# Sixteen outer rows for wq and the FFN up weights, and a gate load of which 896 columns come in two transfers of their own

## The chip, the cores and the metric

The kernel runs on one core of a Trainium2 chip. The metric is the device time in microseconds (us) of one execution. Most executions of one kernel agree within a few tenths of a per cent (30 of the 37 runs of the kernel before lie within 0.35% of 120.8 us, all of them at 120.45 to 121.83); some are slower (two of six of the changed kernel) and are then marked slow, and a single run has an unknown state. Times are compared between fast runs. The "span" of a profiled run is what its trace covers, about 2 us less than its time (118.8 of 121.36 us for the kernel before).

## The reference, cut to what matters

It is one decode step: layer norm, attention over the last 1024 positions of a cache, and a gated FFN, multiplied together.

```python
x  = A_x                                   # 8 x 1 x 512, bf16
xn = _layernorm(x)
q  = xn @ wq                               # wq 512 x 4096
# ... softmax(q k^T) v over the last 1024 positions, 8 KV heads of 128 ...
s  = o @ wo                                # wo 4096 x 512
g  = _silu((_gelu(xn @ w_gate) * (xn @ w_up)) @ w_down)   # gate, up 512 x 1792
return x + s * g
```

With one token per sequence there is little arithmetic for each byte. The bytes are 4.2 MB of wq, 33.6 MB of K and V, 5.5 MB of FFN weights (gate, up and down) and 4.2 MB of wo, 47.46 MB in all, and every one is read once.

## The kernel before

A load of wq, gate or up gives each of the 128 partitions four consecutive rows of the weight (`k=NDC`, NDC is 4), so a partition's piece is one contiguous run in HBM: 16 KB for half of wq's columns of those rows, 14 KB for gate or up.

```python
wq_rows = A_wq.rearrange("(p k) n -> p (k n)", k=NDC)

def load_wide(rows, c0, c1):
    t = wide_slot()
    nc.sync.dma_start(out=t[:, 0 : c1 - c0], in_=rows[:, c0:c1])
    return t

def load_wq(h):                            # h = 0, 1: half of each partition's run
    return load_wide(wq_rows, h * 2 * Hq * Dh, (h + 1) * 2 * Hq * Dh)

def load_up(w):                            # gate and up
    return load_wide(w.rearrange("(p k) n -> p (k n)", k=NDC), 0, NDC * F)
```

A K or V tile holds four heads, `HN`. Its source is already in two levels, 32 outer rows by 4 heads of 8 KB each:

```python
def load_kv(cache, b, i):
    t = slot()
    nc.sync.dma_start(out=t, in_=cache[b, i*HN:(i+1)*HN, win0:Sk, :].rearrange(
        "n (p r) d -> p n (r d)", r=NKR))
    return t
```

The row order of the weights has to be the order of the contracted elements of the normalised input, which is transposed in four steps:

```python
nc.vector.tensor_scalar(out=xhat, in0=x_sb, scalar1=mv[:, 0:1], scalar2=rstd[:, 0:1], ...)
for k in range(NDC):
    nc.tensor.transpose(xT_ps[:, k, :],
                        xhat.rearrange("b (p k) -> b k p", k=NDC)[:, k, :],
                        ident[0:32, 0:32])
```

All large loads are issued by one queue, in this order: first half of wq, a K tile, second half of wq, a K tile, then V and K tiles in turn, and at the end gate, up, down and wo in six pieces from large to small. Tiles free up behind the computation, and the loads wait for them.

The softmax here doesn't subtract the row's maximum and nothing guards it: scores larger than these inputs give would overflow.

Of the kernel before, what the change touches and what calls it, by code (L numbers as in the profile page):

```python
# [16 lines left out]
def kernel(  # L17
# [13 lines left out]
    nc = tc.nc  # L31
# [7 lines left out]
    F = B_w_gate.shape[1]  # L39
    NDC = D // 128  # L40
# [4 lines left out]
    P = nc.NUM_PARTITIONS  # L45
# [33 lines left out]
    def wide_slot():  # L79
        return wide.tile([P, 2 * SLOT], BF16, name="wide_slot", align_bytes=512)  # L80
# [5 lines left out]
    x_sb = persist.tile([32, D], BF16, name="x_sb")  # L86
# [3 lines left out]



    wq_rows = A_wq.rearrange("(p k) n -> p (k n)", k=NDC)

    def load_wide(rows, c0, c1):
        t = wide_slot()
        nc.sync.dma_start(out=t[:, 0 : c1 - c0], in_=rows[:, c0:c1])
        return t

    def load_wq(h):  # L100
# [4 lines that stand above are left out]
        nc.sync.dma_start(  # L105
            out=t,
            in_=cache[b, i * HN : (i + 1) * HN, win0:Sk, :].rearrange(
                "n (p r) d -> p n (r d)", r=NKR
            ),
        )  # L110
        return t

    def load_up(w):
        return load_wide(w.rearrange("(p k) n -> p (k n)", k=NDC), 0, NDC * F)

    def load_down():
        return load_wide(B_w_down.rearrange("(p j) d -> p (j d)", j=FR), 0, FR * D)
# [4 lines left out]
    def load_wo(j0, j1):  # L122

        if (j1 - j0) * D > SLOT:
            return load_wide(wo_rows, j0 * D, j1 * D)
        t = slot()
        nc.sync.dma_start(out=t[:, 0 : (j1 - j0) * D], in_=wo_rows[:, j0 * D : j1 * D])
        return t
# [14 lines left out]
    for t in range(2):  # L143
        c = slice(t * D // 2, (t + 1) * D // 2)
# [6 lines left out]
        out=ident,  # L151
        in_=ident,
# [8 lines left out]
        out=perm.rearrange("p (h q) -> p h q", q=P // 32),  # L161
        in_=ident.rearrange("p (q h) -> p h q", q=P // 32),
# [9 lines left out]
        out=hot.rearrange("n r (m j) -> n r m j", m=HN),  # L172
        in_=hot.rearrange("n r (m j) -> n r m j", m=HN),
# [9 lines left out]
        out=far.rearrange("n (c m) -> n c m", m=HN),  # L183
        in_=far.rearrange("n (c m) -> n c m", m=HN),
# [9 lines left out]
        out=selq,  # L194
        in_=ident.rearrange("p (m q) -> p q m", q=QW),
# [5 lines left out]
        out=selr.rearrange("p r q -> p (r q)"),  # L201
        in_=ident.rearrange("p (u c) -> p c u", u=4),
# [10 lines left out]
    nc.vector.reciprocal(out=rstd, in_=rstd)  # L213
    xhat = persist.tile([32, D], BF16, name="xhat")
    nc.vector.tensor_scalar(  # L215
        out=xhat,
        in0=x_sb,
        scalar1=mv[:, 0:1],
        scalar2=rstd[:, 0:1],
        op0=ALU.subtract,  # L220
# [3 lines left out]
    for k in range(NDC):  # L224
        nc.tensor.transpose(  # L225
            xT_ps[:, k, :],
            xhat.rearrange("b (p k) -> b k p", k=NDC)[:, k, :],
            ident[0:32, 0:32],
        )
    xT = persist.tile([P, NDC, 32], BF16, name="xT")  # L230
# [20 lines left out]
    def turn_k(g, t):  # L251

        kp = ps_t.tile([P, 4 * P], FP32, name="t_ps", tag="t")
        kw = k_t[g].bitcast(FP32)
        for c in range(4):
            rp = 4 * t + c
            nc.tensor.transpose(  # L257
                kp[:, c * P : (c + 1) * P], kw[:, rp * P : (rp + 1) * P], ident_f
            )
        if t == 0:  # L260
            kT_t[g] = kT_pool.tile([P, NKR * P], BF16, name="kT")
        copy = nc.scalar.copy if t == 1 else nc.vector.tensor_copy
        copy(out=kT_t[g][:, t * 8 * P : (t + 1) * 8 * P], in_=kp.bitcast(BF16))  # L263
# [3 lines left out]
    def score(g):  # L267

        b, i = groups[g]
        sc = ps_sc.tile([P, 512], FP32, name="sc_ps")  # L270
        sc_t[g] = sc
        kT = kT_t[g].rearrange("w (r k e) -> w r k e", k=P, e=2)
        nc.tensor.matmul(  # L273
            sc,
            hot.rearrange("n r q -> n (r q)"),
            far,
            start=True,
            stop=False,
            skip_group_check=True,
        )  # L280
        for e in range(2):
            for t in range(4):
                nc.tensor.matmul(  # L283
                    sc[32 * t : 32 * t + 32, :],
                    q2_all[:, i, b, e, :, :, :].rearrange("w r n j -> w (r n j)"),
                    kT[:, :, 32 * t : 32 * t + 32, e],
                    start=False,
                    stop=(e == 1),
                    skip_group_check=True,
                    tile_position=(0, 32 * t),  # L290
                )

    def soft(g):
        p = p_pool.tile([P, 512], BF16, name="p")
        acc = small.tile([P, 1], FP32, name="acc")
        nc.scalar.activation(  # L296
            out=p, in_=sc_t[g], func=ACT.Exp, scale=inv_sqrt_dh, accum_out=acc
        )
        p_t[g] = p, acc

    def turn_p(g):
        p, acc = p_t[g]
        pT = pT_pool.tile([P, 512], BF16, name="pT")
        nc.vector.transpose(out=pT, in_=p)  # L304
        pT_t[g] = pT
        if g % 2 == 0:
            ss_t[g] = small.tile([P, 2, QW], FP32, name="ss")
        nc.vector.tensor_scalar(
            out=ss_t[g - g % 2][:, g % 2, :], in0=selq, scalar1=acc[:, 0:1], scalar2=None, op0=ALU.mult
        )  # L310

    def values(g):

        o_ps = ps_o.tile([P, 2 * Dh], FP32, name="o_ps")
        for m in range(NKR // 2):
            u = m % 4
            nc.tensor.matmul(  # L317
                o_ps[32 * u : 32 * u + 32, :],
                pT_t[g][:, m * 32 : (m + 1) * 32],
                v_t[g][:, m * 256 : (m + 1) * 256],  # L320
                start=(m < 4),
                stop=(m >= NKR // 2 - 4),
                skip_group_check=True,
                tile_position=(0, 32 * u),
            )
        o_sb = o_pool.tile([P, 2 * Dh], FP32, name="o_sb")
        nc.scalar.copy(out=o_sb, in_=o_ps)  # L327
        o_t[g] = o_sb
# [81 lines left out]
    for i in range(NHALF):  # L410
        for rr in range(2):
            copy = nc.scalar.copy if rr else nc.vector.tensor_copy
            copy(
                out=q_sb[:, i, :, :, rr, :],
                in_=q_ps[i].rearrange("p (j w e) -> p j e w", j=rep, e=2),
            )
    for i in range(NHALF):
# [8 lines left out]
        for e in range(2):  # L426
            for rr in range(2):
                copy = nc.scalar.copy if rr else nc.vector.tensor_copy
                copy(  # L429
                    out=q2_all[64 * rr : 64 * rr + 64, i, :, e, rr, :, :].rearrange(  # L430
                        "p b n j -> p j n b"
                    ),
                    in_=qT_ps[64 * rr : 64 * rr + 64, :, e, :, 0:32:NQ],
# [82 lines left out]
    for g in range(NGR + 1):  # L516
        if g < NGR:
            v_t[g] = load_kv(A_v_cache, *groups[g])
            if g + 2 < NGR:
                k_t[g + 2] = load_kv(A_k_cache, *groups[g + 2])  # L520
        if g == NGR - 1:
            wg_t = load_up(B_w_gate)
            wu_t = load_up(B_w_up)
            wd_t = load_down()
        if g == NGR:

            parts = [(0, 16), (16, 24), (24, 28), (28, 30), (30, 31), (31, 32)]
            wo_t = [load_wo(*q) for q in parts[:2]]
            for t in range(2):
                r = slice(16 * t, 16 * t + 16)  # L530
                nc.sync.dma_start(out=x_res[r, :], in_=x_rows[r, :])
            wo_t += [load_wo(*q) for q in parts[2:]]
        if g < NGR:
            score(g)
            soft(g)
        if g + 1 < NGR:
            turn_k(g + 1, 0)
        if g < NGR:
            turn_p(g)
        if g + 1 < NGR:  # L540
            turn_k(g + 1, 1)
        if g:
            values(g - 1)
        if g + 1 < NGR:
            turn_k(g + 1, 2)
            turn_k(g + 1, 3)
        if g and g % 2 == 0:
            gather(g - 2)
# [11 lines left out]
    for pair in [(j, j + 1) for j in range(0, NOR - 2, 2)] + [(NOR - 2,), (NOR - 1,)]:  # L560
        for q in range(NQ):
            for j in pair:
                a = side[j]
                rows = [m for m in range(NOR) if side[m] == a]
                piece, j0 = where[j]
                c0 = (j - j0) * D + q * DQ
# [17 lines left out]
        out=out.flatten_outer_dims().rearrange("b (q c) -> (b q) c", q=NQ), in_=out_sb  # L584
# [31 lines left out]
```

## Time and profile before

| | before |
|---|---|
| time, median of 3 | 120.66 us (120.59 to 120.96) |
| span of the profiled run | 118.8 us |
| second half of wq landed; q matmuls start | 15.46 us; 15.50 us |
| gate landed | 97.11 us |
| up landed | 101.35 us |
| last piece of wo landed | 115.50 us |
| duration of a data packet: 16 KB, 14 KB, 8 KB | 611, 535, 309 ns |

### The profile page before, as it was taken

What the parts mean: (1) busy time and instruction counts of PE and PEld (TensorE: products, weight loads), DVE (VectorE), ACT (ScalarE), POOL (GpSimd) and SP (SyncE); (2) the same over time, 40 slices, a digit from 0 to 9 for tenths busy, and PEclk for the clock granted to TensorE, in tenths of its full rate; (3) what the DMA queues carried; (4) which work ended last, traced back from release to release, by engine and by line L of the source; (5) the groups of instructions that cost most, each with busy time, mean ns of one, the idle gap of its engine ahead of it and who ended that gap; (6) DMA issues with size and microseconds to landing.
All of it is one profiled execution on the core that took longest, in us unless ns stands there. A gap on an engine that the chain in (4) does not pass through costs nothing.

```text
span 118.8 us, 2378 instructions
## 1 busy us (share of the span) xinstructions
PE 86.6 (73%) x985; PEld 59.4 (50%) x985; DVE 62.0 (52%) x131; ACT 40.5 (34%) x78; POOL 4.8 (4%) x14
## 2 busy tenths in 40 slices
PE   0005946786989899799799798778959661898680
PEld 0004713653657567577477386456638340334670
DVE  5025645543756856956866764846728336420111
ACT  5000324792442552462462462442524303002000
POOL 5900000000000000000000000000000000000000
PEclk9999999555899999999999999999999996579999
DMA  4999999999999999999999999999999999999950
GB/s 88 437 394 436 419 433 425 422 433 419 428 428 430 422 417 436 417 430 428 419 422 436 425 417 433 428 425 425 422 428 446 419 449 415 440 438 400 409 193 3
DMA packets 6345, 47.61 MB, mean 401 GB/s; under 512 B 816, under 2 KB 1088, under 8 KB 1344
## 3 DMA queue, kind: packets, MB, share of 16 engines
q1 hardware_dynamic: 6304, 47.47, 95.3%
q8 instruction: 7, 0.11, 0.3%
q14 instruction: 2, 0.02, 0.0%
q10 hardware_dynamic: 32, 0.01, 0.0%
HBM read 47.46 MB, written 0.01 MB: 400 GB/s over the span
## 4 chain that ended last, share of the span: by engine, by line
DMA 58%; PE 24%; DVE 7%; ACT 4%; SPq 2%; issue 1%; DVEq 0%
DMA wide_slot<-in_B_w_gate_dram 18%; DMA slot<-in_A_v_cache_dram 16%; DMA slot<-in_A_wo_dram 12%; DMA wide_slot<-in_A_wq_dram 11%; PE t_ps L257 11%; DVE kT L263 4%; PE sc_ps L283 4%; PE o_ps L317 3%; ACT q_all L429 2%; PE a_ps L344 2%; DVE q_all L429 2%; PE big L567 1%; ACT L296 1%; PE sc_ps L273 1%; PE big L445 1%
## 5 line engine op out<-in xcount | busy, mean ns | idle before, releaser
L263 DVE COPY kT<-t_ps 128x1024 bf16<-128x1024 bf16 x48 | 31.7, 688 | 23.3 <-PE t_ps L257 21.4
L257 PE MATMUL t_ps<-ident_f,slot 128*128 128x128 f32 x256 | 38.3, 300 | 2.4 <-DMA slot<-in_A_k_cache_dram 2.2
L257 PEld LDWEIGHTS t_ps<-ident_f,slot 128*128 128x128 f32 x256 | 31.1, 153 | 12.5 <-issue 7.6
L263 ACT COPY kT<-t_ps 128x1024 bf16<-128x1024 bf16 x16 | 16.2, 1012 | 11.6 <-ACT p L296 5.0
L296 ACT ACTIVATE p<-sc_ps 128x512 bf16<-128x512 f32 x16 | 9.6, 597 | 30.1 <-PE sc_ps L283 30.0
L283 PE MATMUL sc_ps<-kT,q_all 128*32 128x512 bf16 x128 | 10.7, 406 | 7.6 <-DVE kT L263 5.8
L304 DVE STREAM_TRANSPOSE pT<-p 128x512 bf16<-128x512 bf16 x16 | 11.2, 703 | 2.7 <-ACT p L296 2.7
L317 PE MATMUL o_ps<-slot,pT 128*32 128x256 bf16 x256 | 9.9, 275 | 1.1 <-DVE pT L304 1.1
L344 PE MATMUL a_ps<-selr,o_sb 128*128 128x16 f32 x64 | 8.4, 263 | 0.0
L283 PEld LDWEIGHTS <-q_all 128*32 128x32 bf16 x128 | 2.0, 95 | 12.4 <-DVE kT L263 8.4
L344 PEld LDWEIGHTS a_ps<-selr,o_sb 128*128 128x128 f32 x64 | 7.8, 192 | 0.0
L225 PE MATMUL t_ps<-ident,xhat 32*128 32x32 bf16 x4 | 0.3, 194 | 10.3 <-DVE xhat L215 10.3
L317 PEld LDWEIGHTS <-pT 128*32 128x32 bf16 x256 | 5.4, 95 | 4.2 <-issue 2.5
L327 ACT COPY o_sb<-o_ps 128x256 f32<-128x256 f32 x16 | 6.0, 377 | 1.3 <-PE o_ps L317 1.3
L273 PE MATMUL sc_ps<-far,hot 4*128 4x512 bf16 x16 | 6.4, 398 | 0.0
L445 PE MATMUL big<-wide_slot,xT 128*32 128x448 bf16 x32 | 2.6, 463 | 4.3 <-DMA wide_slot<-in_B_w_up_dram 3.1
L225 PEld LDWEIGHTS <-xhat 32*128 32x128 bf16 x4 | 0.2, 114 | 10.2 <-DVE xhat L215 10.2
L567 PEld LDWEIGHTS <-og 128*32 128x32 bf16 x128 | 4.1, 97 | 2.2 <-issue 1.1
L366 PE MATMUL t_ps<-q_sb,ident 128*32 128x512 bf16 x14 | 4.8, 497 | 0.0
L353 DVE RECIPROCAL rs<-a_ps 128x32 f32<-128x32 f32 x8 | 2.9, 358 | 3.0 <-PE a_ps L344 3.0
L429 DVE COPY q_all<-t_ps 64x128 bf16<-64x128 bf16 x4 | 2.7, 778 | 2.4 <-ACT q_all L429 1.6
L429 ACT COPY q_all<-t_ps 64x128 bf16<-64x128 bf16 x4 | 2.7, 726 | 2.5 <-DVE q_all L429 2.5
(70 smaller groups left out, 54.2 us busy)
## 6 DMA issues: line engine op xcount, KB each, us to landing
slot<-in_A_k_cache_dram SPq DMA_DIRECT2D x16, 1024.0 KB, 19.6
slot<-in_A_v_cache_dram SPq DMA_DIRECT2D x16, 1024.0 KB, 19.6
wide_slot<-in_A_wq_dram SPq DMA_DIRECT2D x2, 2048.0 KB, 10.6
wide_slot<-in_A_wo_dram SPq DMA_DIRECT2D x1, 2048.0 KB, 12.3
wide_slot<-in_B_w_gate_dram SPq DMA_DIRECT2D x1, 1792.0 KB, 21.4
wide_slot<-in_B_w_up_dram SPq DMA_DIRECT2D x1, 1792.0 KB, 23.2
wide_slot<-in_B_w_down_dram SPq DMA_DIRECT2D x1, 1792.0 KB, 25.0
slot<-in_A_wo_dram SPq DMA_DIRECT2D x1, 1024.0 KB, 14.4
```

The lines of the kernel that those rows point to most:

```text
L257: nc.tensor.transpose(kp[:, c * P : (c + 1) * P], kw[:, rp * P : (rp + 1) * P], ident_f)
L263: copy(out=kT_t[g][:, t * 8 * P : (t + 1) * 8 * P], in_=kp.bitcast(BF16))
L273: nc.tensor.matmul(sc, hot.rearrange("n r q -> n (r q)"), far, start=True, stop=False, skip_group_check=True,)
L283: nc.tensor.matmul(sc[32 * t : 32 * t + 32, :], q2_all[:, i, b, e, :, :, :].rearrange("w r n j -> w (r n j)"), kT[:, :, 32 * t : 32 * t + ...
L296: nc.scalar.activation(out=p, in_=sc_t[g], func=ACT.Exp, scale=inv_sqrt_dh, accum_out=acc)
L304: nc.vector.transpose(out=pT, in_=p)
L317: nc.tensor.matmul(o_ps[32 * u : 32 * u + 32, :], pT_t[g][:, m * 32 : (m + 1) * 32], v_t[g][:, m * 256 : (m + 1) * 256], start=(m < 4), st ...
L327: nc.scalar.copy(out=o_sb, in_=o_ps)
L344: nc.tensor.matmul(a_ps[:, 1, m, :], o_t[g + m][:, r * Dh : (r + 1) * Dh], selr[:, r, :], start=(r == 0), stop=(r == 1), skip_group_check= ...
L366: nc.tensor.matmul(idle[0:32, :], ident[:, 0:32], moving[:, 0:512], start=True, stop=True, skip_group_check=True,)
L429: copy(out=q2_all[64 * rr : 64 * rr + 64, i, :, e, rr, :, :].rearrange("p b n j -> p j n b"), in_=qT_ps[64 * rr : 64 * rr + 64, :, e, :, 0 ...
L567: nc.tensor.matmul(acc[a], shifted(og, j, q), wo_t[piece][:, c0 : c0 + DQ], start=(j == rows[0] and q == 0), stop=(j == rows[-1] and q == ...
```

## The change

The intent was balance. When gate lands, eight of the DMA engines finish up to 1.4 us later than the other eight. A transfer whose outer dimension is 8 runs on eight engines only (in the trace of the kernel before each load of the 8 rows of x leaves 8 completion marks), so some bytes of the gate weight were to be given to one set of eight. To get an outer dimension of 8 over 64 partitions, the rows of wq, gate and up take another order: partition `8a + c` holds the four rows that start at `(16c + a) * 4`. The source of a 128-partition load then has 16 outer rows by 8.

```diff
-    wq_rows = A_wq.rearrange("(p k) n -> p (k n)", k=NDC)
+    def blocks(w):
+        return w.rearrange("(c a k) n -> a c (k n)", c=8, k=NDC)
+
+    wq_rows = blocks(A_wq)
 ...
-        nc.sync.dma_start(out=t[:, 0 : c1 - c0], in_=rows[:, c0:c1])
+        nc.sync.dma_start(out=t[:, 0 : c1 - c0], in_=rows[..., c0:c1])
 ...
-    def load_up(w):
-        return load_wide(w.rearrange("(p k) n -> p (k n)", k=NDC), 0, NDC * F)
+    def load_up(w, low=0):
+        rows, n = blocks(w), NDC * F
+        t = load_wide(rows, 0, n - low)
+        if low:
+            for a in range(0, 16, 8):
+                nc.sync.dma_start(
+                    out=t[8 * a : 8 * a + 64, n - low : n], in_=rows[a : a + 8, :, n - low : n]
+                )
+        return t
 ...
-        out=xhat,
-        in0=x_sb,
+        out=xhat.rearrange("b (k a c) -> b c a k", a=16, c=8),
+        in0=x_sb.rearrange("b (c a k) -> b c a k", a=16, c=8),
 ...
-            xhat.rearrange("b (p k) -> b k p", k=NDC)[:, k, :],
+            xhat[:, k * P : (k + 1) * P],
 ...
-            wg_t = load_up(B_w_gate)
+            wg_t = load_up(B_w_gate, 896)
```

The bytes and the shapes of the matmuls stay the same. So does the length of each contiguous run, except that gate's 14 KB runs are cut into 12.25 and 1.75 KB.

## The prediction

Passages that rest on more than this case's traces and runs are cut out of the recorded texts, here and below, and the cuts are marked. "Low" engines are my name for the eight that carry the loads of the 8 rows of x, "high" for the other eight; no record numbers an engine, so that another load of 8 or of 4 rows runs on the same ones was not shown.

> **What bounds the kernel now.** I read the shares of the 40 slices first. The engines' row of busy time (tensor engine 73%, VectorE 52%) names no bound; the DMA row does.
>
> ```profile
> DMA  4999999999999999999999999999999999999950
> GB/s 88 437 394 436 419 433 425 422 433 419 428 428 430 422 417 436 417 430 428 419 422 436 425 417 433 428 425 425 422 428 446 419 449 415 440 438 400 409 193 3
> ...
> HBM read 47.46 MB, written 0.01 MB: 400 GB/s over the span
> ```
>
> All 16 DMA engines are over 90% busy from the second slice to the 38th, at some 425 GB/s. All of the 47.46 MB has to come in; nothing but the last landing and what follows it sets the end. The chain of work that ended last, in order of time, says what follows:
>
> ```profile
> 99.92 14.42 DMA slot<-in_A_wo_dram
> 114.33 0.04 issue
> 114.37 1.56 PE big L567 x32
> 115.94 0.02 issue
> 115.96 0.29 DVE tmp L581
> 116.25 0.02 issue
> 116.27 0.28 DVE out_sb L582
> ```
>
> The last pieces of wo arrive, matmuls that consume them piece by piece, two VectorE operations, the store: a tail of about 3.3 us after the last landing. The matmuls had waited for each piece just before:
>
> ```profile
> 114.37 1.55 PE L567 MATMUL big<-slot,og 128*32 128x128 bf16 x32 [0.32 <-DMA slot<-in_A_wo_dram]
> ```
>
> So a nanosecond on the DMA engine that finishes last is a nanosecond on the kernel, and the mean over engines does not matter. The gate load itself (the chain charges it 21.41 us) is queueing: it was issued at 75.69 and landed at 97.11, and the tensor engine sat 1.18 us idle for it there, but what waits on it (the GELU) is done long before the last wo piece (the FFN's result is ready at 110.5).
>
> Therefore I looked **engine by engine**. Each transfer leaves up to 16 completion marks in the trace's semaphore records, one per DMA engine. For the second wq load they lie within 0.3 us. For the gate load eight lie at 95.42 to 95.68 us and eight at 96.16 to 97.11; for the last wo piece eight at 113.90 to 114.13 and eight at 114.60 to 115.50. Half of the engines run about 1.4 us late, half are idle that long at the end. What makes them late is in the queue table and the packet records:
>
> ```profile
> q1 hardware_dynamic: 6304, 47.47, 95.3%
> q8 instruction: 7, 0.11, 0.3%
> q14 instruction: 2, 0.02, 0.0%
> q10 hardware_dynamic: 32, 0.01, 0.0%
> ```
>
> The seven packets of q8 are 16 KB each and start at 27.2, 42.0, 54.1, 67.0, 81.8, 92.5 and 112.3 us. Each hits one engine: it takes 0.95 us, and the data packet behind it 0.76 to 0.85 us in place of 0.31, so that engine is about 1.4 us late ever after. The number of late marks grows with them: 1 after the first, 3 after the second (a q14 packet of 8 KB came 0.5 us before it), and 8 by 97 us.
>
> [...]the x_sb loads of 8 rows show 8 data completions, and their 16 packets of 512 B on q10 fall on 8 engines.[...] No record of this trace holds addresses[...].
>
> **The change part by part.**
>
> *Intent.* In the new row order the last 896 columns have a source of 8 outer rows by 8, [...]both transfers run on the eight low engines. That takes bytes from the high eight and gives them to the low eight. It pays if the high eight are the late ones.
>
> *Are they?* I followed each engine through the packet records: a packet starts 3 or 4 ns before the end of the one before it, so chains of packets can be strung together, and the eight that carry the q10 packets are the low ones. Of the eight late engines at the gate landing, I get low ones for the fetches at 54.1 and 67.0 us and for the q14 packet at 41.5; high ones for 27.2, 42.0, 81.8 and 92.5; the q14 packet at 60.4 is ambiguous (two chains in the same phase). So three or four low engines and four or five high ones are late. The split is not low against high. The last landings of the low late ones and of the high late ones are equal to within about 0.3 us.
>
> *Cost per engine.* Median packet times are 46 ns for 1024 B, 84 for 2048, 309 for 8192 and 535 for 14336, with 3 ns of overlap. By interpolation (an estimate) 1792 B steps by 71 ns and 12544 B by 467. Gate on one engine before: 8 x 532 + 6 (completion) = 4.26 us. After, a low engine: 8 x 467 + 16 x 71 + 18 = 4.89 us, that is **+0.63 us**; a high engine: 8 x 467 + 6 = 3.74, **-0.52 us**. The late high engines gain half a microsecond, the late low ones lose 0.63, and the end follows the low ones: +0.3 (if they are the earlier of the late) to +0.63, my middle +0.5 us.
>
> *Issue.* Two more issues on the sync queue at about 0.4 us each. At this point that queue has waited 2 us per issue for a completion and then 16.2 us for the gate tile, so nothing shows. The eight completion semaphores are handed out in turn; the two small loads push up and down two turns (some 5 us) later, to about 83 and 85.5 us, still 15 us ahead of their data. The two last wo pieces still wait for up and down, as before. Nothing.
>
> *Row order.* The same bytes in rows of the same length (16 KB of wq, 14 KB of up); packet count: 128 gate packets of 14336 B become 128 of 12544 and 128 of 1792. The K and V loads already have a two-level source (32 by 4) and run at 309 ns for 8 KB, full rate. So no loss from a strided source is expected. The xhat operation (0.40 us, at 9.8 us) writes through a four-level pattern; even at three times that, xT is ready 0.8 us later and the first transposes of K (at 10.65) slip, but the q matmuls wait for the second wq half at 15.50, and DMA has the bound anyhow. Nothing.
>
> Sum: 120.66 + 0.5 = **121.1 us**.
>
> **Rivals.** *The low engines are early, as the change assumes.* Then every late engine gains 0.52 and the early ones stay below them (1.4 > 0.63 + 0.52): 120.1 us. For it: the split is exactly eight and eight. Against: my tracking, in which the engines of 54.1 and 67.0 us are clear low ones with no near neighbour of the other kind just before the fetch. It could also come true if the fetches fall on other engines in other executions, which one trace cannot show.
>
> [...]wq, gate and up (7.7 MB) could run at down to half their rate: the wq pair, 4 MB at 425 GB/s or 9.9 us, up to twice as long, gate and up (8.6 us) somewhat less because the late engines are out of step. +5 to +14 us, 126 to 135 us. [...]Against: K and V, whose 32 by 4 source may be split the same way, show no loss. One chance in six.
>
> *Hidden anyway.* If the end were set by the tensor engine, nothing would move: 120.7. Against: it idles for the last wo pieces.
>
> **Range and chances.** Fetches as in this trace (about three in five) give 120.9 to 121.4; other fetch patterns 120.0 to 121.4[...]. Range 120.0 to 122.4. Faster by over 2% needs 2.4 us, more than the whole spread of the engines: 0.01. Slower by over 2% is the collision: 0.15. Within 2%: 0.84.
>
> **What would show it.** In the changed kernel's profile: the gate packets in two sizes (12544 and 1792 B); on the small loads 8 completions only; in the last wo piece's marks a wider spread, about 2.5 us from first to last in place of 1.6, if low engines are among the late, or a narrower one, about 0.5 us, if the first rival holds. wq packets of 16 KB at 611 ns would refute the collision, 900 ns or more confirm it; the second wq landing (15.50 now) would move from the start. The prediction is wrong if the row order slows DMA, or if instruction fetches land on other engines than I read.

## More of the kernel before

For this case another view is the most useful: stretches of the execution with the rate of each. In its lines come the stretch (start:end, then its length, in us), the busy time of each engine, the tensor engine's granted clock, the mean busy share of the 16 DMA engines, and last the GB/s. For the kernel before:

```profile
2.50:7.00 4.50, 0.00 (x0) 0.00 (x0) 0.57 (x3) 0.00 (x0) 3.53 (x8) 1.00 0.90 384
10.00:15.00 5.00, 4.63 (x36) 3.74 (x37) 2.90 (x6) 1.01 (x1) 0.00 (x0) 1.00 1.01 433
15.60:90.00 74.40, 63.29 (x687) 43.58 (x685) 46.60 (x91) 33.95 (x65) 0.00 (x0) 0.93 1.01 426
91.00:101.50 10.50, 5.13 (x79) 3.52 (x82) 5.41 (x13) 2.44 (x6) 0.00 (x0) 0.87 1.01 429
```

The lines are the first half of wq (with the start of the queue), the second half, the K and V tiles, and gate with up. Apart from the start, each kind of load moves at the same 426 to 433 GB/s.

## The result, and the profile after

| | before | after |
|---|---|---|
| time, median of 6 | 120.71 us (120.59 to 121.34) | 140.91 us (139.67 to 142.21) |
| ratio | | 1.1625 (95% interval 1.1569 to 1.168) |
| second half of wq landed | 15.46 us | 25.78 us |
| gate landed | 97.11 us | 112.71 us |
| up landed | 101.35 us | 120.91 us |
| last piece of wo landed | 115.50 us | 134.69 us |

A ratio here and below is the mean time of one kernel's fast runs over that of the other's fast runs of the same rounds, so it is not quite the ratio of the medians. Two of the six runs of the changed kernel (141.99 and 142.21 us) count as slow and are left out of the ratio. The profiled run of the changed kernel was a fast one. From its page, the DMA row and the rate of each of the 40 slices (3.46 us each now), and the queue table:

```profile
DMA  4999999999999999999999999999999999999930
GB/s 114 218 210 254 324 213 192 355 421 431 433 414 426 433 426 412 429 436 417 419 438 426 414 429 436 421 419 433 426 288 239 254 240 215 323 446 412 406 112 2
...
q1 hardware_dynamic: 6448, 47.47, 94.7%
...
HBM read 47.46 MB, written 0.01 MB: 343 GB/s over the span
```

The engines look exactly as busy as before, 94.7% against 95.3%, and the bytes are the same. What changed is the second row. In slices 2 to 4, in 6 and 7, and from 30 to 34 the same busy engines move about half as much. **A busy share counts time in which a packet is open, not bytes.** The stretches make it sharp:

```profile
2.50:12.00 9.50, 0.00 (x0) 0.00 (x0) 0.57 (x3) 0.00 (x0) 3.53 (x8) 1.00 0.98 214
12.50:14.50 2.00, 0.00 (x0) 0.00 (x0) 0.99 (x3) 0.29 (x1) 0.00 (x0) 1.00 0.90 369
15.00:25.00 10.00, 4.89 (x36) 3.89 (x37) 3.92 (x6) 1.01 (x1) 0.00 (x0) 0.93 0.99 210
27.00:100.00 73.00, 62.63 (x678) 43.28 (x671) 46.54 (x90) 33.88 (x65) 0.00 (x0) 0.93 1.01 426
101.00:121.00 20.00, 6.55 (x79) 3.83 (x83) 5.60 (x14) 2.44 (x6) 0.00 (x0) 0.70 1.01 254
121.00:132.00 11.00, 10.19 (x116) 5.38 (x116) 2.10 (x4) 0.85 (x2) 0.00 (x0) 0.78 0.99 412
```

In order: first half of wq, the K tile between the halves, second half of wq, K and V, gate with up, down with wo. Exactly the three weights in the new order are slow; the K tile between two slow loads recovers at once (369 GB/s with both changeovers in the stretch). The chain of waits puts the same loss at two places and then ends as before:

```profile
2.17 23.61 DMA wide_slot<-in_A_wq_dram
25.82 1.50 PE big L413 x9
...
90.66 22.05 DMA wide_slot<-in_B_w_gate_dram
...
115.13 18.30 DMA slot<-in_A_wo_dram
133.47 0.62 PE big L580 x16
134.11 1.07 PE big L580 x16
```

(The lines of the changed file are 13 further down: L413 is the old L400, L580 the old L567.) The first line was `1.92 13.54` before. The landings give the sum: the second half of wq is late by 10.3 us, gate by 15.6 and up by 19.6, so 5.3 and 4.0 more, and the last piece of wo by 19.2. That is about 10 us from wq and about 9 from gate and up, together the whole difference.

The single packets, from the trace's records (median ns):

| packets | before | after |
|---|---|---|
| wq, 16 KB, second half | 611 | 1279 |
| K and V, 8 KB | 309 | 309 |
| gate, 14336 B before, 12544 B after (469 without a collision, experiment 9) | 535 | 851 |
| up, 14336 B | 535 | 1012 |
| the two small loads, 1792 B (74 without a collision, experiment 9) | | 114 |
| wo, 16 KB | 611 | 611 |

116 of the 128 packets of the second half of wq took over 1000 ns; before it was none.

### The profile page after: what moved, and what is told of

It reads as the page before. It is cut to its first block, busy times and chain, and to the rows that moved or that the text cites. A ratio compares the mean times of both kernels' runs of the same rounds, so it can differ in the third digit from the quotient of the medians.

```text
span 138.4 us, 2381 instructions
## 1 busy us (share of the span) xinstructions
PE 89.2 (64%) x985; PEld 60.2 (43%) x985; DVE 63.3 (46%) x131; ACT 40.5 (29%) x78; POOL 4.8 (3%) x14
## 3 DMA queue, kind: packets, MB, share of 16 engines
q1 hardware_dynamic: 6448, 47.47, 94.7%
## 4 chain that ended last, share of the span: by engine, by line
DMA 60%; PE 23%; DVE 7%; ACT 4%; SPq 2%; issue 1%; DVEq 0%
DMA wide_slot<-in_A_wq_dram 17%; DMA wide_slot<-in_B_w_gate_dram 16%; DMA slot<-in_A_v_cache_dram 14%; DMA slot<-in_A_wo_dram 13%; PE t_ps L270 10%; DVE kT L276 5%; PE sc_ps L296 3%; PE o_ps L330 3%; ACT q_all L442 2%; PE a_ps L357 2%; DVE q_all L442 2%; PE big L580 1%; PE big L413 1%; ACT L309 1%; PE t_ps L434 1%
## 5 line engine op out<-in xcount | busy, mean ns | idle before, releaser
L270 PE MATMUL t_ps<-ident_f,slot 128*128 128x128 f32 x256 | 37.8, 297 | 2.3 <-DMA slot<-in_A_k_cache_dram 2.2
L270 PEld LDWEIGHTS t_ps<-ident_f,slot 128*128 128x128 f32 x256 | 30.5, 151 | 11.9 <-issue 7.2
L458 PE MATMUL big<-wide_slot,xT 128*32 128x448 bf16 x32 | 3.9, 571 | 11.8 <-DMA wide_slot<-in_B_w_up_dram 7.3
L458 PEld LDWEIGHTS <-xT 128*32 128x32 bf16 x32 | 1.3, 124 | 13.6 <-issue 12.6
L413 PE MATMUL big<-wide_slot,xT 128*32 128x512 bf16 x32 | 3.0, 507 | 4.7 <-DMA wide_slot<-in_A_wq_dram 4.7
L222 DVE BATCH_NORM_STATS2 stats<-x_sb 32x6 f32<-32x512 bf16 x1 | 0.7, 682 | 10.0 <-DMA x_sb<-in_A_x_dram 10.0
L580 PEld LDWEIGHTS <-og 128*32 128x32 bf16 x128 | 4.2, 97 | 1.5 <-issue 0.9
## 6 DMA issues: line engine op xcount, KB each, us to landing
slot<-in_A_k_cache_dram SPq DMA_DIRECT2D x16, 1024.0 KB, 19.6
```

Source lines behind the costliest of these rows:

```text
L270: nc.tensor.transpose(kp[:, c * P : (c + 1) * P], kw[:, rp * P : (rp + 1) * P], ident_f)
L458: nc.tensor.matmul(ps[32 * j : 32 * j + 32, 0:FT], xT[:, k, :], ws[:, k * F + j * FT : k * F + (j + 1) * FT], start=(k == 0), stop=(k == N ...
L580: nc.tensor.matmul(acc[a], shifted(og, j, q), wo_t[piece][:, c0 : c0 + DQ], start=(j == rows[0] and q == 0), stop=(j == rows[-1] and q == ...
```

## The experiments

Four theories could account for packets of twice the duration, and they were told apart in this order.

- **Small loads:** the two transfers on eight engines are to blame.
- **HBM order (H):** neighbouring partitions now come from places 512 KB apart in HBM.
- **Destination (P):** engines that write certain partitions at the same moment hold each other up; a source of 16 outer rows makes them meet, one of 32 does not. How a load is spread over the engines and where they would meet was my guess; no record shows it, so the runs can only tell which loads are slow. P has a *local* form, in which only the engines that meet are slow, and a *global* one, in which a few that meet hold up all sixteen.
- **xhat's pattern:** VectorE needs longer. This one fell on reading alone: the operation went from 0.40 to 1.58 us, but it ended at 16.1 us, and the q matmuls waited for wq until 25.82.

### 1. The row order without the small loads

```diff
-            wg_t = load_up(B_w_gate, 896)
+            wg_t = load_up(B_w_gate)
```

> The new row order with 16 outer rows by 8, but the gate weight in one transfer, no small transfers on eight engines. Theory P[...]: wq packets of 16 KB stay at about 1280 ns, the second wq half lands near 25.8 us, time 139 to 141 us. Theory H (rows far apart in HBM are slow to read): the same. Theory S (the two small transfers on eight engines are what costs): back to 120.7 us. The small transfers alone cost at most 1 us in P and H.

Measured: 139.80 us (138.39 to 140.94, 4 runs), ratio 1.1536 (1.1476 to 1.1597). The row order alone makes nearly all of the difference. The two small loads seem to be worth the rest, about 1 us (the ratios 1.1625 and 1.1536 differ by 0.9%), but the intervals of the two ratios overlap, so that this is not clear of noise.

### 2. The same idea with 32 outer rows

The kernel of experiment 1 with partitions in runs of four: the source has 32 rows by 4, as K and V have, and neighbouring partitions of wq lie 1 MB apart in HBM, further than in the changed kernel.

```diff
-        return w.rearrange("(c a k) n -> a c (k n)", c=8, k=NDC)
+        return w.rearrange("(c a k) n -> a c (k n)", c=4, k=NDC)
 ...
-        out=xhat.rearrange("b (k a c) -> b c a k", a=16, c=8),
-        in0=x_sb.rearrange("b (c a k) -> b c a k", a=16, c=8),
+        out=xhat.rearrange("b (k a c) -> b c a k", a=32, c=4),
+        in0=x_sb.rearrange("b (c a k) -> b c a k", a=32, c=4),
```

> A row order with 32 outer rows by 4 in place of 16 by 8; neighbouring partitions are then twice as far apart in HBM (1 MB in wq). No small transfers. Theory P: [...]wq packets 611 ns, second wq half lands at 15.5 us, time 120.4 to 121.2 us. Theory H: as slow as the changed kernel or slower, 139 us or more. Theory S says 120.7 too, so this run decides between P and H only.

Measured: 121.06 us (120.95 to 122.47, 6 runs), ratio 1.0045 (1.0004 to 1.0086). wq packets take 611 ns again. Its stretches, the end of the first half of wq with the K tile behind it, the second half, K and V, gate:

```profile
5.00:9.80 4.80, 0.00 (x0) 0.00 (x0) 0.85 (x2) 0.20 (x1) 1.04 (x6) 1.00 0.95 405
10.20:15.00 4.80, 3.26 (x18) 3.23 (x19) 3.08 (x5) 1.01 (x1) 0.00 (x0) 1.00 1.01 434
15.60:92.40 76.80, 66.42 (x723) 46.12 (x726) 49.10 (x95) 34.49 (x66) 0.00 (x0) 0.96 1.01 427
92.40:97.20 4.80, 3.70 (x50) 2.85 (x42) 1.04 (x4) 1.32 (x4) 0.00 (x0) 0.75 1.02 430
```

Theory H falls: a source scattered over 1 MB steps runs at the full rate. The strided source as such is innocent too, and so is the pattern of xhat (1.57 us here). What is left is the number of outer rows, 16 against 32.

### 3. The old row order, each half of wq in two transfers of 64 partitions

If the destination is the cause, then the row order is not needed at all. My estimate was that a load into 64 partitions at a time, 0 to 63 or 64 to 127, is enough for the loss.

```diff
-        return load_wide(wq_rows, h * 2 * Hq * Dh, (h + 1) * 2 * Hq * Dh)
+        t = wide_slot()
+        c = slice(h * 2 * Hq * Dh, (h + 1) * 2 * Hq * Dh)
+        for r in (slice(0, 64), slice(64, 128)):
+            nc.sync.dma_start(out=t[r, :], in_=wq_rows[r, c])
+        return t
```

> The kernel before, row order untouched, but each wq half loaded in two transfers of 64 partitions (0 to 63, then 64 to 127). All 16 engines work on each[...]. Theory P[...]: wq packets of 16 KB at about 1250 ns in place of 611, second wq half lands near 25 us in place of 15.5, time 130 to 131.5 us; all from the destination, as the source rows are read in the old order. Theory H (the order of rows in HBM): nothing changes, 120.7 us. A rival that only an outer dimension of 16 is slow: 120.7 us too.

Measured: 131.76 us (131.47 to 131.99, 4 runs), ratio 1.0886 (1.0842 to 1.093). The second half of wq and K with V:

```profile
15.00:25.00 10.00, 5.81 (x36) 3.93 (x36) 2.80 (x5) 1.01 (x1) 0.00 (x0) 1.00 1.02 215
27.00:85.00 58.00, 51.33 (x524) 35.06 (x517) 36.64 (x71) 26.67 (x51) 0.00 (x0) 0.86 1.01 426
```

The same 215 GB/s and the same packets (1264 to 1280 ns in the median) as in the changed kernel, with rows in the old order and neighbouring partitions 32 KB apart. Each transfer is now 1 MB in place of 2, but that is no cause by itself: a K or V load is 1 MB too and runs at 426 GB/s. Writing 64 partitions at a time is enough for the loss.

### 4. wq alone in the new order

Experiment 1 with gate and up in the old order. The FFN's result is then wrong, since xhat is in the new order. (It passed the comparison with the reference all the same. An estimate of why: with random inputs of the reference's scales, `s * g` has a standard deviation of about 0.0001 beside 0.05 for `x`, so the comparison hardly sees it. It is then no test of the row order in the other runs either; that the patterns of x and of the weights agree there is read off the code.)

```diff
-        rows, n = blocks(w), NDC * F
+        rows, n = w.rearrange("(p k) n -> p (k n)", k=NDC), NDC * F
```

> Only wq (and x) in the 16 by 8 row order; gate and up in their old order, so the result is wrong on purpose and only the time counts. It splits the loss between wq and the FFN weights. From the traces, the second wq half lands 10.3 us later in the changed kernel: if that share is carried to the end unchanged, 130.5 to 131.5 us here, and the other half of the loss (8 to 9 us) belongs to gate and up. If the delay of wq were partly hidden behind other work: under 129 us.

Measured: 131.65 us (130.79 to 131.69, 4 runs), ratio 1.0857 (1.0805 to 1.091), with all up packets at 535 ns. So by the ratios wq costs 10.4 us (8.6% of 121), and gate with up another 8.2 (experiment 1's 15.4% less 8.6%), which agrees with the landings.

### 5. Engines out of step

The prediction had said that gate and up would lose less because some engines run late. Here four engines get eight packets of 8 KB each ahead of the second half of wq, to put them behind the others, in the kernel of experiment 1.

```diff
+    lag = wide_slot()
+    lag_rows = A_wo.rearrange("(c a j) d -> a c (j d)", c=8, j=Hq * Dh // P)
+    nc.sync.dma_start(out=lag[4:36, 0:SLOT], in_=lag_rows[0:4, :, 0:SLOT])
     wq_t += [load_wq(1)]
```

> As the rows-only run (16 by 8), plus one extra load of 256 KB on four engines alone (source 4 outer rows), between the first K tile and the second wq half: it puts the four lowest engines eight packets of 8 KB (2.5 us) behind, which is half of the eight 16 KB packets that an engine has of a wq half. Theory P: in the second wq half [...]64 of its 128 packets take 611 to 700 ns, the other 64 (the high engines, not staggered) stay near 1280; the 128 of the first half all stay near 1280. The time hardly moves (139 to 142 us), as the high engines still end last. Theory H: all 256 packets stay near 1280 ns.

Measured: 144.11 us, above the 139 to 142 expected, and no fast half: 116 of the 128 packets of the second half took over 1000 ns, as in the changed kernel. This refuted what I had expected of the local form. The trace shows something else in its place. From 24.5 to 28.8 us only the four late engines still worked on wq; the other twelve had gone on to a K tile, whose 8 KB packets had never been slow:

```profile
15.00:24.50 9.50, 5.72 (x36) 4.06 (x37) 4.12 (x6) 1.01 (x1) 0.00 (x0) 1.00 1.01 222
24.50:28.80 4.30, 0.00 (x0) 0.00 (x0) 0.00 (x0) 0.00 (x0) 0.00 (x0) 0.67 1.00 217
29.50:40.00 10.50, 7.90 (x53) 4.86 (x53) 4.72 (x7) 4.82 (x7) 0.00 (x0) 0.50 1.01 425
```

In the middle stretch the K packets took 633 ns in the median (467 to 649), against 309, and the rate stayed at 217 GB/s. Only four of the sixteen engines were still at work on the slow load, and yet no K packet kept its 309 ns. That is the global form, and the next pair was made to test it.

### 6. A pair: four engines with extra work, into partitions 0 to 15 and into 64 to 79

The kernel before with one extra load of 256 KB on four engines ahead of the second half of wq (it adds 20 packets to the queue, 6324 for 6304: 16 of data and 4 completions). The twins differ in the destination alone.

```diff
+    lag = wide_slot()
+    lag_rows = A_wo.rearrange("(c a j) d -> a c (j d)", c=4, j=Hq * Dh // P)
+    nc.sync.dma_start(out=lag[D0 : D0 + 16, 0:8192], in_=lag_rows[0:4, :, 0:8192])
     wq_t += [load_wq(1)]
```

`D0` is 0 in the first twin and 64 in the second. I expected no collision in the first and one in the second; that was a guess about which engine writes which partitions in the other loads, and no record holds addresses. The second recorded text also had a third outcome, as the twin, if the destination does not matter.

> The kernel before plus one extra load of 256 KB on four engines (source 4 rows by 4, 16 KB each), between the first K tile and the second wq half, into partitions 0 to 15[...]. Theory P: no collision; the four packets of each of these engines take about 611 ns, so do the wq packets of the others; those four engines are 2.44 us later for good, which is 1.0 us beyond the late ones if they are on time ones, 2.4 if one of them is late: 121.7 to 123.2 us.

> The same extra load, same source, same four engines, but into partitions 64 to 79[...]. Two forms of theory P. Local: [...]about 16 of the 128 packets of the second wq half, plus the 16 extra ones, go to about 1220 ns and the other engines stay at 611. Global: [...]about 48 of the 128 wq packets at 1000 ns or more during some 5 us. Time 123 to 125.7 us in both, against 121.7 to 123.2 of the twin run.[...]

Measured, partitions 0 to 15: 122.78 us (122.48 to 123.19, 4 fast runs), ratio 1.0137 (1.009 to 1.0184), all packets of that stretch 611 ns. Partitions 64 to 79: one fast run of four, 124.92 us, and a profile in the slow state, so I ran it again:

> The run[...] once more, as its profile fell in the slow state and its packets stayed at 352 ns in place of 309 for 70 us after the extra load was over. If that after-effect belongs to the collision: again runs over 128 us among those near 125, none of them in the kernel before. If it was a passing disturbance of the chip: all runs 123 to 125.7 us. In both cases some 48 of the wq packets take 1000 ns or more (the global form of theory P).

Measured: fast runs 124.71, 124.80 and 125.28 us, ratio 1.0325 (1.0278 to 1.0372); the other three, the profiled one among them, were slow. The stretch that holds the second half of wq, partitions 0 to 15:

```profile
10.60:15.20 4.60, 4.60 (x28) 3.70 (x32) 2.80 (x5) 1.01 (x1) 0.00 (x0) 1.00 1.02 436
```

and partitions 64 to 79, with the stretch after it:

```profile
10.60:15.20 4.60, 4.33 (x25) 3.57 (x28) 2.70 (x5) 1.01 (x1) 0.00 (x0) 1.00 0.99 224
15.20:86.00 70.80, 55.12 (x542) 36.96 (x535) 36.74 (x72) 27.33 (x52) 0.00 (x0) 0.86 1.01 377
```

(In the repeat the first stretch has 228 GB/s.) Of the 144 packets of the load (128 of wq and the extra 16) 55 took over 1000 ns, and 54 in the repeat. Over the same 144 the local form had asked for some 32 (16 of wq and the 16 extra), the global one for some 64 (48 and 16). The start times decide it: every packet that started between 10.65 and 13.3 us took 1220 ns or more (42 packets, 37 in the repeat), where the local form leaves the other engines at 611. **The extra load of four engines, moved from partitions 0 to 15 to 64 to 79, halved the rate of all sixteen**, as long as it lasted (224 in place of 436 GB/s). Both profiles are slow runs, so the fast runs have to confirm it: 4.6 us at 224 in place of 436 GB/s lose 4.6 x (1 - 224/436) = 2.2 us, and the fast runs are slower than the twin's 122.78 by 1.9 to 2.5 us.

The second line is a surprise that stays open. From the end of the collision (15 us) to about 95 us nearly every packet took 1.14 times as long as before: 700 ns in place of 611 for the rest of wq, 352 in place of 309 for K and V. Both profiles show it, but both are slow runs, and the 9 us by which their spans exceed the fast runs' 123.1 is about what 352 against 309 ns makes of these 80 us. It may well be that the slow runs alone have it. Six of the ten runs of this kernel were slow, and none of the 13 of the kernel before that ran beside them; by what was written before the repeat (runs over 128 us among those near 125, none in the kernel before), the slow runs then go with the collision. Why, and why only some executions have it, is not known: no fast run was profiled.

### 7. Extra work for the eight low engines, into partitions 0 to 31

This tests the arithmetic of the prediction, free of a collision. It adds four packets of 4 KB to each low engine of the kernel before.

```diff
+    lag = wide_slot()
+    lag_rows = A_wo.rearrange("(c a j) d -> a c (j d)", c=4, j=Hq * Dh // P)
+    nc.sync.dma_start(out=lag[0:32, 0:2048], in_=lag_rows[0:8, :, 0:2048])
     wq_t += [load_wq(1)]
```

> The kernel before plus an extra load of 128 KB on the eight low engines only (source 8 rows by 4, 4 KB each), into partitions 0 to 31[...]. It gives each low engine 0.63 us more and takes nothing from the high ones: the one step of my prediction that the collision hid. If low engines are among the late ones: 121.2 to 121.4 us (ratio about 1.005). If only high ones are late (the intent of the change): below the lead of 1.4 us, so 120.7 us (1.000).

Measured: 121.34 us (121.22 to 121.74, 6 runs), ratio 1.0031 (0.9998 to 1.0063). All wq packets stay at 611 ns. In the trace the last mark of the last wo piece moves from 115.50 to 116.11 us, +0.61, and its 16 marks spread over 2.15 us in place of 1.60. The times only lean the same way: the interval still holds 1. One trace's marks scatter too: experiment 2, with no extra bytes, has its last mark at 115.80 us.

### 8. The same eight engines, in runs of eight partitions

The destination is partitions 0 to 63. The cut differs, eight outer rows of eight partitions, and with it the size: 64 packets of 4 KB in place of 32. The size alone was expected to give 121.9 to 122.1 us (the second outcome of the recorded text, whose condition is cut: that the cut makes no difference).

```diff
-    lag_rows = A_wo.rearrange("(c a j) d -> a c (j d)", c=4, j=Hq * Dh // P)
-    nc.sync.dma_start(out=lag[0:32, 0:2048], in_=lag_rows[0:8, :, 0:2048])
+    lag_rows = A_wo.rearrange("(c a j) d -> a c (j d)", c=8, j=Hq * Dh // P)
+    nc.sync.dma_start(out=lag[0:64, 0:2048], in_=lag_rows[0:8, :, 0:2048])
```

> The kernel before plus an extra load of 256 KB on the eight low engines (source 8 rows by 8, 4 KB each) into partitions 0 to 63, in place of 8 rows by 4 into partitions 0 to 31[...]. It asks how the load is cut. If by whole outer rows[...]: [...]the 64 extra packets of 4 KB take near 320 ns in place of 159, and about 30 to 60 of the 128 wq packets beside them 1000 ns or more; 122.5 to 124.5 us, possibly more in the slow state. [...]159 ns, no slow wq packet, 121.9 to 122.1 us, and theory P would have to be given up.

Measured: 123.19 us (122.91 to 123.89, 4 runs), ratio 1.021 (1.0159 to 1.0261), on the 2% line, so unclear as a verdict. Before, during and after the extra load:

```profile
8.00:10.50 2.50, 0.31 (x4) 0.21 (x4) 1.40 (x4) 0.29 (x1) 0.00 (x0) 1.00 1.03 421
10.50:12.80 2.30, 1.80 (x10) 1.80 (x10) 1.37 (x3) 0.00 (x0) 0.00 (x0) 1.00 1.02 262
12.80:16.00 3.20, 3.20 (x25) 2.06 (x24) 1.43 (x3) 1.01 (x1) 0.00 (x0) 1.00 1.05 448
```

The extra packets took 206 ns in the median (159 in experiment 7), and 20 of the 128 wq packets over 1000 ns. So there is a collision that experiment 7 did not have. I put it down to the cut into runs of eight; as partitions 32 to 63 are new here too, the pair does not show which of the two it is. I had expected more of it: 64 extra packets near 320 ns, and 30 to 60 slow wq packets. The first 25 of the extra packets were still at 159 ns, and later ones went up to 322; why it sets in late is not known. No record holds addresses, so how a load is cut among the engines was not shown.

### 9. The intent, without the slow row order

The row order of experiment 2 (with its lines for xhat, left out below) keeps the full rate, and a source of 8 rows by 4 can be cut out of it as well: four transfers of 32 partitions for the last 896 columns of gate.

```diff
-        return w.rearrange("(c a k) n -> a c (k n)", c=8, k=NDC)
+        return w.rearrange("(c a k) n -> a c (k n)", c=4, k=NDC)
 ...
-            for a in range(0, 16, 8):
+            for a in range(0, 32, 8):
                 nc.sync.dma_start(
-                    out=t[8 * a : 8 * a + 64, n - low : n], in_=rows[a : a + 8, :, n - low : n]
+                    out=t[4 * a : 4 * a + 32, n - low : n], in_=rows[a : a + 8, :, n - low : n]
                 )
```

> The intent of the change without its split: rows in the 32 by 4 order, and the last 896 gate columns in four transfers of 32 partitions, source 8 by 4, so that they still run on the eight low engines. Theory P: no collision, so what is left is the shift of half a microsecond from the high to the low engines. If low engines are among the late ones, as I read in the trace of the kernel before: 121.0 to 121.4 us, and the last wo piece's completion marks spread over about 2.2 to 2.6 us in place of 1.6. If only high engines are late: 120.1 to 120.3 us. Theory H: 139 us or more.

Measured: 123.32 us (123.06 to 124.03, 6 runs), ratio 1.0224 (1.0194 to 1.0254): missed by some 2 us. The stretches before, during and after the third and fourth small transfer:

```profile
90.80:96.10 5.30, 4.20 (x63) 3.22 (x62) 2.55 (x6) 1.40 (x5) 0.00 (x0) 1.00 1.01 421
96.10:99.20 3.10, 1.64 (x17) 0.85 (x17) 1.00 (x3) 0.00 (x0) 0.00 (x0) 0.62 1.02 302
99.20:104.50 5.30, 2.17 (x21) 0.96 (x19) 2.58 (x5) 1.12 (x2) 0.00 (x0) 0.50 1.01 430
```

The first 64 small packets, into partitions 0 to 63, took 74 ns each. The other 64, into partitions 64 to 127, took 98 in the median and up to 142, and up's packets, on their way on the other engines, about 800 in place of 535. (Each of the four transfers leaves 8 completions: the queue has 6464 packets for 6304, 128 of them of data.) It looks like experiment 6 again, inside the intent: again a load on some of the engines left the rate alone in the low partitions (421 GB/s) and not from partition 64 on (302). Of the 2.3 us over experiment 2, that stretch makes 3.1 x (1 - 302/430) = 0.9, and the shift of bytes some 0.6 (experiment 7); 0.7 us I did not trace.

No version tried beats the kernel before. A further idea, a source of 16 outer rows from neighbouring places in HBM, was not run; experiments 2 and 3 answer its question from the other side.

## Why the prediction was right or wrong

- **The bound: right.** The DMA engines set the end before and after, and the tail after the last landing is the same (133.47, then 0.62 and 1.07 us of matmuls).
- **"So no loss from a strided source is expected": the step that failed.** It carried the whole error. The step compared wq, gate and up with K and V because both have a source in two levels, and did not compare the outer dimension, 16 against 32. With 32 the step would have held: in experiment 2 wq moves at 434 and gate at 430 GB/s, and the cost is 0.4%. With 16 a packet of wq takes 1279 ns in the median in place of 611.
- **Half the rate for wq, gate and up: the right rival, given one chance in six, and sized at 5 to 14 us; it was 20.** What makes the engines collide was not shown; that the destination counts, experiment 6 shows (224 in place of 436 GB/s). It was refused by the same faulty comparison ("K and V, whose 32 by 4 source may be split the same way, show no loss"). Its term for wq was right: "up to twice as long", 9.9 us, measured 10.3 (the landing) and 10.4 (experiment 4). Its term for gate and up was too small: "somewhat less because the late engines are out of step". They took 8 to 9 us more, on top of the 8.6 us before. The upper end of 14 was too low even for the prediction's own terms: twice as long for both is 9.9 + 8.6 = 18.5 us. (And wq, gate and up are 7.9 MB in the units of these sums, not 7.7.) Being out of step does not help (experiment 5), since the collision holds up all engines, also those at work on another load (K packets at 633 ns in experiment 5) and those without extra work (every packet from 10.65 to 13.3 us at 1220 ns or more in experiment 6).
- **Low engines are among the late ones: supported, not proved.** The same +0.63 us per low engine shows as +0.61 at the last landing of one trace (experiment 7); the times alone can't tell it from noise. The first twin of experiment 6 says it more clearly: its four engines got 2.44 us more, which was expected to move the end by 1.0 us if all four were on time, and the last landing moved by 1.87 us (115.50 to 117.37), the time by 1.1 to 2.2 us (its ratio). That these four, or the eight of experiment 7, are low ones was not shown. So the intended balance seems to go the wrong way in this kernel even where no engines collide. In the changed kernel the effect is buried: it is part of the 1 us or so of the two small loads.
- **One reading was off by an engine.** At the last wo piece of the kernel before, seven marks lie at 113.90 to 114.13 us and nine at 114.59 to 115.50, not eight and eight; the end is set by the last of them, so the sum does not change.
- **The spread of the last marks:** foreseen at about 2.5 us with low engines late. It was 3.22 in the changed kernel, whose engines the collisions had moved as well, and 2.15 in experiment 7, which is the clean case; where no low engine has extra work it is 1.60 to 1.89 (the kernel before, experiments 2 to 4).
- **Issue and xhat: right in effect.** xhat took four times as long, more than the three that the prediction allowed, and stayed off the path.
- **The named test worked.** "900 ns or more" for wq packets and a later second wq landing were what would confirm the collision, and both came. How 16 outer rows are cut was something that nothing in the trace of before had shown, and a rival that rests on an unknown of that kind deserved far more than one chance in six.

## What to carry to other kernels

Before a load is reshaped, ask how many outer rows its source has and which partitions it writes at one time, and not only how long the runs are or how many engines take part: in this kernel 32 outer rows were free (434 GB/s) and 16 cost half of the rate (210 to 214). Take an existing load as evidence only if its outer dimension is the same. When the busy share of the DMA engines stays the same and GB/s halve, look at the duration of one packet in a stretch where only one load runs; and be wary of an extra load on a few engines, for here one of 256 KB on four of them made all sixteen wait in partitions 64 to 79 (224 GB/s) and none in 0 to 15 (436).
